# One row list against another: gate products of two chunks read their rows back from DRAM, and fillers, products and route writes change places

## The chip, the cores and the metric

The kernel runs on one core of a Trainium2 chip. The metric is the device time of one launch in microseconds; the median of three runs of the kernel before is 587.76 us (586.64 to 587.94). A profiled execution gives the rows that are read below.

## The reference, cut to what matters

```
phi(x) = exp(x omega^T - |x|^2/2 - max) / sqrt(128)        # q and k, scaled; 4 batches, 8 heads, 576 rows, 64 columns
x      = (phi(q) (phi(k)^T v)) / (phi(q) sum(phi(k)))      # linear attention, 2304 rows of 512
h      = x w_in;  x = (h * clip(h + 3, 0, 6) / 6) w_out    # dense layer, 512 -> 2048 -> 512
score  = x w_skip;  logits = x w_gate                      # 1 + 8 gate products per row
e      = argmax(logits);  p = softmax(logits)[e]
out    = x + p * relu(x w1[e]) w2[e]   where score > 0,    else x
```

## The kernel before

Four batches of attention (pairs of heads, `attention`) make x, transposed, in two parts of rounded floats (`xh` and `xl`). The dense layer goes over five chunks of rows, `CHS = (512, 512, 256, 512, 512)`, and 16 steps f of 128 hidden columns each: the product `mm1` (L710, twelve matmuls), ACT's and DVE's relu6 and splitting (L716 to L731: g, gh, gl), and `mm2` (L741, three matmuls for each 128 rows) into accumulators. While the first chunk runs, ACT and DVE also convert the weights (`cv_*`, L641 to L688), which come in as pairs of words; the remainders of w_in are stored as `wils` and loaded again for the later chunks (`load_wil`, tile wil). Attention of batch 1 stands between the products of the first chunk, that of batches 2 and 3 between those of the second and third.

After a chunk's last step, `after(c)` copies each 128 rows from the accumulator into a row buffer x1 (`x1_copy`, ACT, L747; there are three buffers), stores them twice (`x1_out`, SP: to out and to x1d, a table of rows in DRAM), and takes nine gate products of them on DVE (`gate_dot`, L756: a multiply and sum over 512 columns into lg). Then comes the routing of the chunk (`route_*`; `route_put` writes the route table tab from POOL, L834). With four chunks routed, the expert with the most rows (`group`, steps `ga_*`) and a side block (`s_*`) are worked on, their rows fetched from x1d and their results written by POOL (L910, L933), while the fifth chunk ends.

Nothing of this order is found at run time. Each step is registered by `sc.add` with its engine, a cost, its reads and writes, and the buffers it holds; the string `ORDER` numbers the steps in the order in which `Schedule.run` emits them, and every engine takes its own in that order. On all engines a step waits for the ones before it on the same engine, and for its data and buffers. SP issues most loads and stores in the same way.

One thing is emitted by the way. A step "warm" takes a PSUM bank (`warm.append(pacc())`), and until the step that clears it `warm_up` (L292 to L300) puts filler matmuls on the zero tile idle in front of each PE step: `OPEN = 7` of them (14 matmuls in the trace) until the planner's own gap in front of a step is over 0.1, after that as many as fit into that gap. The fillers have no cost in the planner, and the place of the two steps in `ORDER` is as free as that of any other.

```
for _ in range(int((gap - 0.1) / AT["fill"]) if len(warm) > 1 else OPEN):
    T.matmul(warm[0][:, 0:128], idle, idle, start=True, stop=True)
```

## Time and profile before

| what | before |
|---|---|
| median of 3 runs (lowest, highest) | 587.76 us (586.64, 587.94) |
| the profiled execution's own time, and its span | 585.66 us, 583.7 us |
| mean granted TensorE clock in the span | 0.994 |
| busy: PE, DVE, ACT, POOL | 564.7, 422.1, 292.4, 107.7 us |
| HBM read and written | 61.62 MB, 15.18 MB |

The span goes from the first to the last instruction; the own time has what lies around it as well. A busy engine is not always one that paces the others: PE's matmuls are pipelined, so their durations overlap, and start to start is the measure of its pace. Times in the rows are microseconds from the start of the span.

### The profile page before, as it was taken

The page shows a single profiled execution, that of the slowest core. Times are in us where ns is not written, and L with a number is a line of the kernel's source. Part 1 is how long each engine was busy: PE and PEld are TensorE (multiplying, and loading weights), DVE is VectorE, ACT ScalarE, POOL GpSimd, SP SyncE. Part 2 cuts the span into 40 slices and gives each one's busy share as a digit, 9 for nine tenths or more (in the row PEclk, how much of TensorE's full clock was granted, in tenths as well). Part 3 has the DMA queues.
Part 4 walks back from the last instruction along what each step waited for, and adds up shares of the span by engine and source line. Part 5 has one row for each costly group of instructions (what it writes and reads, how often), then busy time and mean ns, then how long its engine had stood idle before and what let it go on. Part 6 is the DMA issues. An engine that isn't in the chain of part 4 may idle for free. (4 is left out here: it accounts for less than half of the span.)

```text
span 583.7 us, 11120 instructions
## 1 busy us (share of the span) xinstructions
PE 564.7 (97%) x4089; PEld 465.3 (80%) x4089; DVE 422.1 (72%) x1116; ACT 292.4 (50%) x665; POOL 107.7 (18%) x83
## 2 busy tenths in 40 slices
PE   6799999999999999999999999999999999999993
PEld 5678787877888788778988888888888888888882
DVE  4998999899968964539889646134489855589881
ACT  5998999998562343238644332121232323552310
POOL 3550221100200202104432002000010035000263
PEclk9999999999999999999999999999999999999997
DMA  8643566566535034215513322213232245473621
GB/s 314 211 151 131 180 232 201 186 195 215 174 135 173 20 123 148 77 48 177 151 57 106 117 68 73 71 38 90 73 83 86 85 128 164 143 230 100 209 68 74
DMA packets 36103, 77.41 MB, mean 133 GB/s; under 512 B 5484, under 2 KB 6124, under 8 KB 36048
## 3 DMA queue, kind: packets, MB, share of 16 engines
q1 hardware_dynamic: 33872, 72.70, 39.2%
q0 software_dynamic: 1744, 3.56, 1.9%
q8 instruction: 33, 0.54, 0.4%
q10 hardware_dynamic: 432, 0.43, 0.3%
q14 instruction: 22, 0.18, 0.1%
HBM read 61.62 MB, written 15.18 MB: 132 GB/s over the span
## 5 line engine op out<-in xcount | busy, mean ns | idle before, releaser
L741 PE MATMUL acc<-wo,gh 128*128 128x512 f32 x576 | 181.3, 396 | 0.0
L741 PEld LDWEIGHTS acc<-wo,gh 128*128 128x128 f32 x576 | 105.4, 188 | 23.9 <-issue 1.9
L756 DVE CUSTOM_DVE_ANT_0 idle<-x,wg 128x512 uint8<-128x512 f32 x162 | 115.2, 711 | 8.6 <-ACT x L747 4.7
L741 PE MATMUL acc<-wo,gl 128*128 128x512 f32 x288 | 112.3, 390 | 0.0
L716 ACT ACTIVATE g<-mm,half_t 128x512 f32<-128x512 f32 (+1 forms) x80 | 51.3, 646 | 84.0 <-PE mm L710 64.0
L549 POOL PARTITION_ALL_REDUCE mx<-pr x26 | 53.2, 2078 | 216.7 <-ACT pr L541 170.0
L731 DVE TENSOR_TENSOR gl<-g,gh 128x512 fp32r<-128x512 f32 (+1 forms) x80 | 51.7, 647 | 49.2 <-ACT gh L725 35.0
L721 DVE SCALAR_TENSOR_TENSOR g<-g,mm 128x512 f32<-128x512 f32 (+1 forms) x80 | 49.8, 629 | 49.5 <-ACT g L716 49.2
L725 ACT CAST gh<-g 128x512 fp32r<-128x512 f32 (+1 forms) x80 | 46.2, 581 | 76.6 <-PE acc L741 64.4
L710 PE MATMUL mm<-xh,wih 128*128 128x512 f32 (+1 forms) x320 | 80.8, 374 | 0.0
L710 PE MATMUL mm<-xl,wih 128*128 128x512 f32 (+1 forms) x320 | 78.8, 368 | 0.0
L710 PEld LDWEIGHTS mm<-xh,wih 128*128 128x128 f32 x320 | 56.2, 188 | 11.5 <-ACT pr L541 0.4
L710 PEld LDWEIGHTS mm<-xl,wih 128*128 128x128 f32 x320 | 56.8, 188 | 10.2
L741 PEld LDWEIGHTS acc<-wo,gl 128*128 128x128 f32 x288 | 54.1, 188 | 11.7
L710 PE MATMUL mm<-xh,wil 128*128 128x512 f32 (+1 forms) x256 | 61.6, 363 | 0.0
L710 PEld LDWEIGHTS mm<-xh,wil 128*128 128x128 f32 x256 | 44.9, 189 | 7.6
L834 POOL DMA_INDIRECT tab<-rec,r_sloti x18 | 18.7, 1042 | 173.1 <-DVE rec L830 169.2
L468 ACT ACTIVATE kp<-att,kmx 128x128 f32<-128x128 f32 x130 | 39.6, 424 | 16.7 <-DVE kmx L453 16.1
L453 DVE TENSOR_REDUCE kmx<-att 128x3 f32<-128x384 f32 (+1 forms) x64 | 28.5, 481 | 8.1 <-PE att L447 8.0
L666 DVE CUSTOM_DVE_ANT_0 ca<-w,ca 128x1024 uint16<-128x1024 uint16 x32 | 24.5, 769 | 3.2 <-ACT w L652 2.3
L447 PE MATMUL att<-wb,raw 64*128 64x128 f32 x260 | 21.1, 295 | 5.1 <-DVE wb L359 4.4
L447 PEld LDWEIGHTS att<-wb,raw 64*128 64x128 f32 x260 | 18.3, 198 | 9.2 <-DVE wb L359 4.4
(220 smaller groups left out, 770.4 us busy)
## 6 DMA issues: line engine op xcount, KB each, us to landing
wil<-wils SPq DMA_DIRECT2D x64, 256.0 KB, 2.8
w<-w_in SPq DMA_DIRECT2D x16, 512.0 KB, 3.6
w<-w_out SPq DMA_DIRECT2D x16, 512.0 KB, 3.4
out<-x SPq DMA_DIRECT2D x18, 256.0 KB, 3.3
x1d<-x SPq DMA_DIRECT2D x18, 256.0 KB, 3.4
vx<-vn SPq DMA_DIRECT2D x13, 322.5 KB, 4.7
wils<-cl SPq DMA_DIRECT2D x16, 256.0 KB, 4.1
wraw<-w SPq DMA_DIRECT2D x16, 256.0 KB, 3.1
```

Source lines behind the costliest of these rows:

```text
L447: T.matmul(st[key, b, p, g, h][:, i * M:(i + 1) * M], x[half(h), min(c * 128, S - 128):min(c * 128 + 128, S)], wb[half(h), :], start=True, ...
L453: V.reduce_max(out=mx[:, 0:n], in_=st[key, b, p, g, h][:, 0:n * M].rearrange("p (g m) -> p g m", m=M), axis=AX.X, negate=True)
L468: A.activation(kp[:, i], ps[:, i * M:(i + 1) * M], AF.Exp, bias=mx[:, i:i + 1], scale=1.0)
L549: G.partition_all_reduce(mx, st["e", b, p, r], channels=128, reduce_op=bass_isa.ReduceOp.max)
L666: V.tensor_tensor(c, c, lo, op=ALU.add)
L710: T.matmul(po, w[:, k, :], moving(x, k, c), start=(n == 0), stop=(n == 3 * KC - 1))
L716: A.activation(t, mmp[c, f][:, 0:CHS[c]], AF.Relu, bias=half_t, scale=2.0 ** -UP / 6.0)
L721: V.scalar_tensor_tensor(out=t, in0=t, scalar=1.0, in1=mmp.pop((c, f))[:, 0:CHS[c]], op0=ALU.min, op1=ALU.mult)
L725: A.copy(gh, gt[c, f])
L731: V.tensor_sub(gl, t, gh.bitcast(F32))
L741: T.matmul(accs[c, t], g[:, ts], w[:, r, f % 2, :], start=(f == 0 and j == 0), stop=(f == FT - 1 and j == 2))
L756: V.tensor_tensor_reduce(out=idle.bitcast(mybir.dt.uint8), in0=x1[i], in1=wg[:, e, :], scale=1.0, scalar=0.0, op0=ALU.mult, op1=ALU.add, a ...
```

## The change

The gate products of chunks 0 and 1 (`LATE`) no longer read the row buffer that ACT has filled, but one that a new step, `x1_in`, loads back from x1d after `x1_out` has stored the rows. The buffer that ACT filled is free when its two stores have landed, and the gate products may stand at any later place before the chunk's routing. The new list has eight steps more (2091 in place of 2083). It moves these products from the second chunk's steps to the end of the third and into the fourth (chunk 0), and into the fourth (chunk 1), and the routing of the chunks with them. It moves most other steps too.

```diff
+LATE = (0, 1)
...
 ORDER = """
-257 258 295 296 333 334 2 259 297 371 261 17 260 267 273 264 274 262 280 269 275 298 270 281 299 276 302 265 277 372
...
+257 258 295 296 17 0 2 333 334 371 259 260 297 32 264 273 262 265 274 280 261 281 298 275 282 276 299 263 302 372 300
...
+    def x1_in(i):
+        xt = x1p.tile([128, DM], F32, tag="x1", bufs=3, name="x1")
+        nc.sync.dma_start(xt, x1d[i * 128:(i + 1) * 128, :])
+        x1[i] = xt
...
-            sc.add("SP", 2 * SPC, t + 1, lambda i=i: x1_out(i), r=[("x1", i)], o=[("wil", (c + 1, 3 + 2 * k))], w=[("x1d", c)], t=[("x1", i)],
+            sc.add("SP", 2 * SPC, t + 1, lambda i=i: x1_out(i), r=[("x1", i)], o=[("wil", (c + 1, 3 + 2 * k))], w=[("x1d", c), ("x1o", i)], t=[("x1", i)],
                    nbytes=128 * DM * 8)
+            again = c in LATE
+            if again:
+                sc.add("SP", SPC, t + AT["dot"] + k * 9 - 5, lambda i=i: x1_in(i), r=[("x1o", i)], w=[("x1i", i)], t=[("x1", ("i", i))], nbytes=128 * DM * 4)
             for e in range(NE + 1):
-                sc.add("DVE", 0.7, ..., lambda i=i, e=e: gate_dot(i, e), r=[("x1", i), "wg"], w=[("lg", c)],
-                       t=[("x1", i)])
+                sc.add("DVE", 0.7, ..., lambda i=i, e=e: gate_dot(i, e), r=[("x1i" if again else "x1", i), "wg"], w=[("lg", c)],
+                       t=[("x1", ("i", i) if again else i)])
```

Lines of the changed kernel are one higher up to the products, and six higher from the gate products on (L298 is L299, L710 is L711, L834 is L840, L910 is L916).

**The start, on ACT and PE.** ACT's first computing steps (L541 copies a query projection, L468 is an exponential of keys), before:

```order
L541 ACT_TABLE_LOAD
L541 COPY pr<-mm 128x288 x2
L468 ACTIVATE kp<-att,kmx 128x128 x2
L541 COPY pr<-mm 128x288 x2
L468 ACTIVATE kp<-att,kmx 128x128 x6
L541 COPY lent_h<-mm 128x288 x2
```

and now:

```order
L469 ACT_TABLE_LOAD
L469 ACTIVATE kp<-att,kmx 128x128 x3
L542 COPY pr<-mm 128x288 x4
L469 ACTIVATE kp<-att,kmx 128x128 x3
L469 ACTIVATE lent_r<-att,kmx 128x128 x3
L542 COPY lent_h<-mm 128x288
```

PE up to the first product of the first chunk (L590 transposes x, L568 makes numerators, L513 and L447 project queries and keys, L298 is the filler), before:

```order
L590 MATMUL mm<-ident,xn 128x128 x10
L568 MATMUL att<-kv,pr 64x65 x20
L513 MATMUL att<-raw,wb 128x288 x2
L298 MATMUL acc<-idle 128x128 x7
L710 MATMUL mm<-xh,wih 128x512 x4
L710 MATMUL mm<-xl,wih 128x512 x4
L710 MATMUL mm<-xh,cl 128x512 x4
```

and now:

```order
L569 MATMUL att<-kv,pr 64x65 x20
L591 MATMUL mm<-ident,xn 128x128 x5
L514 MATMUL att<-raw,wb 128x288 x2
L448 MATMUL att<-wb,raw 128x128 x12
L514 MATMUL att<-raw,wb 128x288 x2
L711 MATMUL mm<-xh,wih 128x512 x4
L711 MATMUL mm<-xl,wih 128x512 x4
L711 MATMUL mm<-xh,cl 128x512 x4
```

An exponential has moved to the front of ACT's list, and the filler no longer stands in front of the first product; two projections of keys and a query projection stand there instead.

**The fillers, on PE.** In the list before, the row above is the only one of L298. In the new list the rows of the filler stand in the first chunk, between second products (acc<-wo) of its steps:

```order
L569 MATMUL att<-kv,pr 64x65 x20
L742 MATMUL acc<-wo,gh 128x512 x2
L742 MATMUL acc<-wo,gl 128x512
L591 MATMUL att<-ident,xn 128x128 x2
L299 MATMUL acc<-idle 128x128 x7
L742 MATMUL acc<-wo,gh 128x512 x2
L742 MATMUL acc<-wo,gl 128x512
L299 MATMUL acc<-idle 128x128 x7
L742 MATMUL acc<-wo,gh 128x512 x2
L742 MATMUL acc<-wo,gl 128x512
L299 MATMUL acc<-idle 128x128 x7
L514 MATMUL att<-raw,wb 128x288 x4
```

Three blocks of seven are emitted where there was one.

**The end, on POOL.** The last writes, before (L834 the route table, L910 a block's rows, L933 the side block's):

```order
L910 DMA out<-xgb,ga_rec 2304x512 x2
L834 DMA tab<-rec,r_sloti 19456x2 x2
L910 DMA out<-xgb,ga_rec 2304x512
L933 DMA out<-xg,s_rec 9216x128
L910 DMA out<-xgc,ga_rec 2304x512 x2
```

and now:

```order
L840 DMA tab<-rec,r_sloti 19456x2 x2
L916 DMA out<-xgb,ga_rec 2304x512 x2
L916 DMA out<-xgc,ga_rec 2304x512
L840 DMA tab<-rec,r_sloti 19456x2
L916 DMA out<-xgc,ga_rec 2304x512
L939 DMA out<-xg,s_rec 9216x128
```

The side block's write has become the last one, and a write of the route table stands between the last two of the blocks' rows. On PE the side block's last steps (L1185, 64 matmuls in the trace) have moved behind the last products of the group.

## Rows read from the trace of the kernel before

**Rows 1.** Page: busy time, share of the span and instructions of each engine.

```profile
PE 564.7 (97%) x4089; PEld 465.3 (80%) x4089; DVE 422.1 (72%) x1116; ACT 292.4 (50%) x665; POOL 107.7 (18%) x83
```

**Rows 2.** Windows: length, then busy us (x instructions) by engine, clock, DMA share, GB/s.

```profile
15.00:30.00 15.00, 11.55 (x225) 9.44 (x224) 13.86 (x29) 14.26 (x40) 7.13 (x4) 1.00 0.57 196
30.00:45.00 15.00, 14.07 (x268) 11.81 (x266) 13.98 (x36) 15.00 (x48) 7.82 (x4) 1.00 0.47 146
...
75.00:90.00 15.00, 15.00 (x145) 12.24 (x143) 13.75 (x31) 15.00 (x33) 2.93 (x2) 1.00 0.62 206
285.00:300.00 15.00, 14.62 (x162) 12.61 (x159) 13.10 (x34) 8.46 (x25) 6.86 (x3) 1.00 0.35 109
...
360.00:375.00 15.00, 15.00 (x68) 12.43 (x67) 7.60 (x18) 2.90 (x5) 1.97 (x3) 1.00 0.20 52
```

**Rows 3.** Page: the gate products (busy, mean ns); the wil loads (KB, us to landing).

```profile
L756 DVE CUSTOM_DVE_ANT_0 idle<-x,wg 128x512 uint8<-128x512 f32 x162 | 115.2, 711 | 8.6 <-ACT x L747 4.7
...
wil<-wils SPq DMA_DIRECT2D x64, 256.0 KB, 2.8
```

**Rows 4.** Timeline of ACT, 0 to 50 us: start, us, what, idle before.

```profile
7.93 0.70 ACT L541 COPY pr<-mm 128x288 f32<-128x288 f32 x2 [4.30 <-PE mm L513]
...
23.51 2.17 ACT L468 ACTIVATE lent_r<-att,kmx 128x128 f32<-128x128 f32 x8
...
27.81 1.43 ACT L652 ACTIVATE w<-w 128x512 f16<-128x512 f32 x1
...
46.26 0.74 ACT L605 CAST xh<-mm 128x192 fp32r<-128x192 f32 x1
```

**Rows 5.** Timeline of DVE: the last xl of batch 0.

```profile
45.52 2.01 DVE L610 TENSOR_TENSOR xl<-mm,xh 128x384 fp32r<-128x384 f32 x5
```

**Rows 6.** Timeline of PE, 47 to 50 us: the fillers and the first product.

```profile
47.52 1.83 PE L298 MATMUL acc<-idle 128*128 128x128 f32 x14
49.11 1.18 PE L710 MATMUL mm<-xh,wih 128*128 128x512 f32 x4
```

**Rows 7.** Timelines of PE and DVE: the first matmuls, the first maximum.

```profile
4.42 2.50 PE L447 MATMUL att<-wb,raw 64*128 64x128 f32 x20 [4.42 <-DVE wb L359]
5.68 0.42 DVE L453 TENSOR_REDUCE kmx<-att 128x2 f32<-128x256 f32 x1 [1.31 <-PE att L447]
```

**Rows 8.** Timeline of PE, 34 to 41 us: prices of attention steps.

```profile
34.92 0.76 PE L513 MATMUL att<-raw,wb 64*128 64x288 f32 x4
...
38.42 0.94 PE L447 MATMUL att<-wb,raw 64*128 64x128 f32 x12
39.30 0.92 PE L484 MATMUL att<-vx,kp 128*64 128x65 f32 x24
```

**Rows 9.** Timelines of ACT and PE near 82 us: an exponential, its numerator product.

```profile
81.75 0.73 ACT L558 ACTIVATE pr<-pr 128x576 f32<-128x576 f32 x1
83.72 1.39 PE L568 MATMUL att<-kv,pr 128*64 128x65 f32 x40
```

**Rows 10.** Timeline of PE, 102 to 106 us: a visit to a half-width shape.

```profile
102.90 0.39 PE L741 MATMUL acc<-wo,gl 128*128 128x512 f32 x1
103.22 1.39 PE L484 MATMUL att<-vx,kp 128*64 128x65 f32 x40
104.54 0.74 PE L741 MATMUL acc<-wo,gh 128*128 128x512 f32 x2
105.11 0.39 PE L741 MATMUL acc<-wo,gl 128*128 128x512 f32 x1
```

**Rows 11.** Timelines of PE and POOL: the side block and the end.

```profile
555.54 1.96 PE L1185 MATMUL acc<-ew,rT 128*32 128x128 f32 x64
573.98 0.39 PE L1059 MATMUL att<-gw,xl 128*128 128x512 f32 x1
574.07 0.97 POOL L910 DMA_INDIRECT out<-xgc,ga_rec  x1 [0.35 <-DVE xgc L1065]
575.43 0.97 POOL L910 DMA_INDIRECT out<-xgc,ga_rec  x1 [0.39 <-DVEq L1583]
```

More of the change, by code (lines that the diff above doesn't have):

```diff
@@ L1432, in after @@
                    t=[("ps", ("acc", c, k)), ("x1", i)])
-            sc.add("SP", 2 * SPC, t + 1, lambda i=i: x1_out(i), r=[("x1", i)], o=[("wil", (c + 1, 3 + 2 * k))], w=[("x1d", c)], t=[("x1", i)],
+            sc.add("SP", 2 * SPC, t + 1, lambda i=i: x1_out(i), r=[("x1", i)], o=[("wil", (c + 1, 3 + 2 * k))], w=[("x1d", c), ("x1o", i)], t=[("x1", i)],
                    nbytes=128 * DM * 8)
+            again = c in LATE
+            if again:
+                sc.add("SP", SPC, t + AT["dot"] + k * 9 - 5, lambda i=i: x1_in(i), r=[("x1o", i)], w=[("x1i", i)], t=[("x1", ("i", i))], nbytes=128 * DM * 4)
             for e in range(NE + 1):
-                sc.add("DVE", 0.7, t + (AT["dot"] if c != CA - 1 else 0) + k * 9 if c < NCH - 1 else t + AT["dot5"] + k, lambda i=i, e=e: gate_dot(i, e), r=[("x1", i), "wg"], w=[("lg", c)],
-                       t=[("x1", i)])
+                sc.add("DVE", 0.7, t + (AT["dot"] if c != CA - 1 else 0) + k * 9 if c < NCH - 1 else t + AT["dot5"] + k, lambda i=i, e=e: gate_dot(i, e), r=[("x1i" if again else "x1", i), "wg"], w=[("lg", c)],
+                       t=[("x1", ("i", i) if again else i)])
         u = t + AT["route5"] if c == NCH - 1 else t + 25 if c == CA - 1 else t + AT["route"]
```

160 rows, old and new, of the table ORDER are left out of this document.

## The prediction

> **What bounds the kernel now.** I read the engine totals first: TensorE (PE) is busy 564.7 of the 583.7 us of the span, the next engine, VectorE (DVE), 422.1 [rows 1]. A total is a mean over stages, so the windows come second [rows 2]. From 75 to 90 us and from 360 to 375 us PE is busy 15.00 of 15.00. It is not from 15 to 45 us (11.55 and 14.07) and, slightly, from 285 to 300 us (14.62). In the early windows it is ScalarE (ACT) that has no room: 14.26 and 15.00 of 15.00 between 15 and 45 us, and 15.00 again from 75 to 90. So the time is made of four things: when PE can begin the products of the first chunk, how much PE work is still to do then, what is added to PE's stream or taken from it after that, and what follows PE's last matmul. From 360 to 375 us that stream holds 68 matmuls of 512 columns in 15.00 us, about 0.225 us each, 2.7 us for a product of twelve.
>
> The gate products are on DVE: 162 of 0.71 us, 115.2 us [rows 3]. Nothing on PE waits for them before the routing, and DVE is busy 7.60 of 15.00 from 360 to 375 us [rows 2]. Moving them later is by itself priced at nothing; the work of PE hides it as long as DVE keeps below 15 in the windows that receive them. What decides is the order on PE, ACT and POOL that came with it.
>
> **Term 1, the first product: -2.5 us.** Before, ACT starts at 7.93 us and runs, nearly without a gap, to the last xh copy at 47.00 [rows 4]; the last xl of DVE ends at 47.53 [rows 5]. The first product starts only at 49.11, because 14 filler matmuls on idle, listed in front of it, begin at 47.52 and take 1.59 us [rows 6]. In the changed list no filler stands there. The ACT work ahead of the last xh copy is also smaller: eight exponentials fewer (eight take 2.17 us) and one L652 more (1.43 us with an overlap of some 0.3 with the next), so 1.0 us less [rows 4]. And ACT's first step is now an exponential of the three-chunk half. Before, PE does the two-chunk half first (8 of the 20 matmuls in 2.5 us), and DVE's first maximum starts at 5.68, some 0.3 us after it, and takes 0.42 [rows 7]. In the changed list the 12 matmuls of the three-chunk half come first, until about 5.8, the maximum follows near 6.1 and takes some 0.5, and ACT starts near 6.9 instead of 7.93. Walking down ACT's new list with these durations I find one new gap, about 1.2 us near 10 us, where the next exponential waits for the next pair's maximum. The last xh copy then ends near 45.2. Four PE steps stand between the last transpose and the first product, so it starts near 46.6, and 49.11 - 46.6 = 2.5. The bounds: -4.4 if ACT has no gap and PE follows at once, and -1.0 if only the filler goes and part of that is lost again.
>
> **Term 2, work done ahead of it: -0.5 us.** Of PE's 53 steps up to the first product the changed list has one more key projection (12 matmuls, 0.94 us), one more query projection (4, 0.76 us) and one k-v product fewer (24, 0.92 us) [rows 8]. That is 0.8 us with the overlaps at their ends; the two projections stand beside others of their shape, so I take 0.5, between 0.3 and 0.8.
>
> **Term 3, new waits for ACT in the first chunk: +1.0 us.** In the changed list four products of 2.7 us stand almost back to back at the start, so PE runs ahead of ACT. For the numerator product of pair 2 of batch 1 the old list has 66 ACT instructions between the last xh copy and the exponential that it needs, the new one 81; PE's own work up to there grows by 4.2 us. In its full window ACT does 33 instructions in 15.00 us [rows 2], so fifteen are 6.8 us, 2.6 more than 4.2. Before, that exponential ended near 82.4 and PE came at 83.72, a margin of 1.3 us [rows 9]. The margin less 2.6, and less 0.7 for the earlier first product, would be a wait of 2.0 us. Where ACT had idled before for want of PE's results the new work fits into the gaps, and the wait would be 0. I take the middle.
>
> **Term 4, the fillers: +4.8 us.** The filler rule emits seven instructions, 14 matmuls in the trace, before each PE step from the one that takes the filler's bank until the clear. In the changed list these two stand in the middle of the first chunk, and three blocks of seven come out, between products of L742 (the order shown with the change). 3 x 1.59 = 4.8 us [rows 6]. PE is busy 15.00 of 15.00 there, so nothing hides them; only a wait of PE that they replace could. The block removed in front of the first product is already in term 1. The lower bound is 2.8, if 2 us of waits for ACT fall behind them.
>
> **Term 5, changes of the array's shape: -1.9 us.** The attention matmuls use half the rows or half the columns of the array, and a visit to one costs more than its matmuls. Around the visit at 103.22 the matmul before it takes 0.32 us instead of 0.225, and the first two after it take 0.57 instead of 0.45; with about 0.06 at the exit that is 0.27 [rows 10]. After the first product the old list returns 28 times from such a visit to a full product, the new one 21 times: 7 x 0.27 = 1.9 (1.1 to 2.5).
>
> **Term 6, the late waits: -0.4 us.** PE's idle time from 285 to 300 us is 15.00 - 14.62 = 0.38 us [rows 2], where DVE is at 13.10 with the attention of batch 3 and the gate products of the second chunk. In the new list DVE has less to do ahead of 270 us. I take the whole of it, with +2 as the other bound: the gate products that now stand from 345 to 435 us bring DVE near 15 of 15 there.
>
> **Term 7, the end: +1.0 us.** Before, PE's last matmul starts at 573.98, and POOL's last write runs from 575.43, 1.45 us later, to 576.40: 2.42 us after that matmul [rows 11]. The changed list ends PE with the eight small steps of the side block (64 matmuls, 1.96 us). Behind the last large product POOL then has four writes in a row: a block's rows, one of the route table, a block's rows, the side block. Each takes 0.97 us, and they follow each other every 1.3 us or so (574.07, 575.43). With the first at 1.45 us after the product before the last, the fourth ends some 6.2 us after it, and PE's own last matmul starts 2.8 us after it. That leaves 3.4 us in place of 2.42. Bounds: 0 and +1.5.
>
> **Reloads: 0.** Eight loads of 256 KB are added on SP's queue. A load of that size (wil, the stored remainders) takes 2.8 us to land [rows 3]; the rows were stored long before. Behind a waiting reload on SP stand the next wil loads, and a product waits for those; they would be PE's next wait (a rival below).
>
> **The sum.** -2.5 - 0.5 + 1.0 + 4.8 - 1.9 - 0.4 + 1.0 = +1.5 us. The profiled execution's own time was 585.66 us, of which 583.7 are the span; the median of the three runs shown is 587.76, 2.1 higher. The terms are differences, so I put them on the median: **589.2 us**, slower by 0.25%. About 0.2%, 1.2 us, is what a measurement of this kernel can tell from no change.
>
> **The rivals.**
>
> *ACT runs through without a gap* (faster, 0.17). If the 1.2 us gap near 10 us does not open and PE is ready when the last xl lands, the first product starts at 44.7 and term 1 is -4.4; PE then meets a filled ACT list and term 3 is 0. The sum is -4.4 - 0.5 + 4.8 - 1.9 - 0.4 + 1.0 = -1.4: 586.4 us. For it: ACT is busy 15.00 of 15.00 from 30 to 45 us [rows 2]. Against it: only 14.26 in the window before, where the first maxima and reductions are waited for. It decides from a first product before 45 us.
>
> *ACT paces the whole first chunk* (no change, 0.14). Then the fillers stand where PE would have waited and cost nothing of their own, and the time up to the second chunk is ACT's work, the same in both lists. The gains of term 5 there are lost too. What is left is about -1.0 from the earlier ACT start, -0.4 and +1.0: 587.4 us. For it: ACT's 15.00 from 75 to 90. Against it: PE was busy 15.00 in that window too [rows 2].
>
> *A reload holds SP's queue* (slower, 0.12). Reloads need one of three row buffers, which a store must release. While one waits, the wil loads behind it wait, and PE with them. PE's work between such a load's place in the list and its product, counted in the third chunk with the durations above, is often only some 3 us, little over the 2.8 us of a landing. If five products lose 0.6 us each, the time is 592.2.
>
> *The clock falls without the filler* (slower, 0.04). The granted clock stayed at 1.00 from 15 to 30 us although PE idled 3.45 us there in pieces [rows 2]. The Trainium skill (TensorE: Matmul & The Clock Gate, Why this matters for your kernels) asks that bursts of matmuls have no long idle gaps between them, or the engine drops to half its rate; by that rule taking the filler away from the first product is a risk, by the row it is none. At 1.2 instead of 2.4 GHz that product would take 2.7 us more: 591.9.
>
> **How the numbers follow.** The forecast's case has 0.53, with an own range of 587.6 to 591.0: slower 0.31, within the bound 0.19, faster 0.03. The first rival gives 0.14 faster and 0.03 within, the second 0.14 within, the last two 0.16 slower. Together: faster 0.17, same 0.36, slower 0.47. The range, 585.6 to 592.0, takes in the first two rivals and the bounds of terms 3 and 6, and leaves out the slow rivals' upper halves.
>
> **What would show it.** Right: the first product near 46.6 us with no L299 in front of it; three blocks of 14 L299 matmuls, some 1.6 us each, between products of L742; short waits of PE for pr, lent or gl between 60 and 85 us; POOL's end some 3.4 us after PE's last matmul starts. Wrong: a first product before 45 or after 48; idle time of PE right in front of the fillers (they would then cost less than 4.8); waits of PE for wil in the third chunk, or for gl from 345 to 435 us.

## The result and the profile after

| what | before | after |
|---|---|---|
| median (lowest, highest) | 587.76 us (586.64, 588.4) | 592.8 us (591.39, 593.3) |
| the profiled execution's own time, and its span | 585.66, 583.7 us | 591.53, 589.7 us |
| mean granted TensorE clock | 0.994 | 0.988 |

The ratio of five timed runs each is 1.0081, with an interval of [1.0061, 1.0101]: slower by 5.0 us on the medians, 5.9 us between the profiled executions. The prediction said 589.2, and its range ended at 592.0. The direction was right, the size was not.

The page after, the lines that answer to [rows 1] and [rows 3]:

```profile
PE 568.7 (96%) x4117; PEld 470.7 (80%) x4117; DVE 424.3 (72%) x1116; ACT 293.0 (50%) x665; POOL 108.1 (18%) x83
...
L762 DVE CUSTOM_DVE_ANT_0 idle<-x,wg 128x512 uint8<-128x512 f32 x162 | 114.4, 706 | 6.7 <-ACT x L748 2.8
...
wil<-wils SPq DMA_DIRECT2D x64, 256.0 KB, 2.7
```

PE has 28 matmuls more and 4.0 us more of busy time; 28 are two blocks of fillers. The gate products cost what they did, and a wil load still lands in 2.7 us. The windows that answer to [rows 2], and three more (90, 300 and 315 us):

```profile
15.00:30.00 15.00, 13.28 (x210) 10.56 (x212) 14.35 (x30) 13.66 (x39) 7.15 (x5) 0.77 0.57 199
30.00:45.00 15.00, 13.83 (x288) 11.59 (x285) 14.55 (x34) 14.97 (x43) 7.08 (x4) 1.00 0.37 121
75.00:90.00 15.00, 15.00 (x144) 12.23 (x142) 14.52 (x30) 14.93 (x34) 2.95 (x2) 1.00 0.74 225
90.00:105.00 15.00, 15.00 (x95) 12.46 (x93) 9.12 (x17) 9.91 (x23) 3.91 (x2) 1.00 0.39 121
285.00:300.00 15.00, 14.89 (x178) 13.46 (x177) 7.73 (x21) 9.06 (x28) 4.69 (x3) 1.00 0.57 170
300.00:315.00 15.00, 14.38 (x121) 11.76 (x120) 12.74 (x32) 6.26 (x16) 4.20 (x3) 1.00 0.53 158
315.00:330.00 15.00, 14.63 (x128) 12.92 (x127) 14.42 (x40) 4.70 (x11) 3.29 (x2) 1.00 0.33 94
360.00:375.00 15.00, 15.00 (x69) 12.28 (x68) 8.38 (x29) 3.21 (x5) 0.00 (x0) 1.00 0.27 83
```

Three things are to be seen. The clock is 0.77 in the mean from 15 to 30 us, where it was 1.00: PE is busy longer there, and its matmuls are slower (shown below). The idle time from 285 to 300 us fell from 0.38 to 0.11 us, and 0.62 and 0.37 us stand in the next two windows. From 90 to 105 us PE is full while ACT and DVE are not. That is where the fillers are, in the timeline of PE:

```profile
48.59 1.20 PE L711 MATMUL mm<-xh,wih 128*128 128x512 f32 x4
...
90.91 1.73 PE L299 MATMUL acc<-idle 128*128 128x128 f32 x14
...
93.18 1.72 PE L299 MATMUL acc<-idle 128*128 128x128 f32 x14
...
95.44 1.72 PE L299 MATMUL acc<-idle 128*128 128x128 f32 x14
```

The first product starts at 48.59, 0.5 us before [rows 6], and three blocks of fillers have come. The end, on PE and on POOL, against [rows 11]:

```profile
574.75 0.39 PE L1065 MATMUL acc<-gw,xl 128*128 128x512 f32 x1
575.07 1.69 PE L1191 MATMUL acc<-ew,rT 128*32 128x128 f32 x38
577.22 0.27 PE L1191 MATMUL acc<-ew,rT 128*32 128x128 f32 x1 [0.46 <-issue]
...
579.35 0.42 PE L1191 MATMUL acc<-ew,rT 128*32 128x128 f32 x4 [1.01 <-issue]
...
580.78 0.67 PE L1191 MATMUL acc<-ew,rT 128*32 128x128 f32 x16 [0.41 <-issue]
```

```profile
578.31 0.97 POOL L916 DMA_INDIRECT out<-xgc,ga_rec  x1 [0.30 <-issue]
582.12 0.97 POOL L939 DMA_INDIRECT out<-xg,s_rec  x1 [2.84 <-DVE xg L944]
```

The 64 small matmuls of the side block took 6.1 us from the start of the first to that of the last, in pieces with idle time between them that nothing in the profile explains ("issue"). POOL stood 2.84 us for them before its last write. In [rows 11] the same 64 are one piece of 1.96 us, some 1.7 from first to last start. All times of this block below are from first to last start.

Term by term, from the two traces, the 6.0 us of the span are:

| term | forecast | measured |
|---|---|---|
| 1, first product | -2.5 | -0.5 |
| 2, work done ahead of it | -0.5 | -0.8 |
| 3, waits for ACT in the first chunk | +1.0 | 0 |
| 4, fillers | +4.8 | +4.6 |
| 5, changes of shape | -1.9 | -1.4 |
| 6, late waits | -0.4 | +1.15 |
| 7, end | +1.0 | +4.0 |
| other | 0 | -1.05 |

Term 7 is the time from the last large product's start to the end of POOL's last write, 8.34 us instead of 2.42, less the 1.88 us of side block matmuls that moved there and are missing elsewhere. "Other" is 0.35 us in small pieces and 0.7 us of span behind POOL's last write. Terms 2 and 5 measure -2.2 together; of that, 0.8 is the price of the moved steps by [rows 8], an estimate. A second profile of the kernel after, on another chip (the run of 589.73 us below), has the same stream of PE to 0.05 us between the first product and the last large one, but its first product starts at 49.95, 0.8 us later than in [rows 6], and its term 7 is +1.5. So terms 2 to 6 repeat, and the two ends do not.

### The profile page after: what moved, and what is told of

Same layout as the page of the kernel before. It is cut to its first block, busy times and chain, and to the rows that moved or that the text cites. A ratio compares the mean times of both kernels' runs of the same rounds, so it can differ in the third digit from the quotient of the medians.

```text
span 589.7 us, 11212 instructions
## 1 busy us (share of the span) xinstructions
PE 568.7 (96%) x4117; PEld 470.7 (80%) x4117; DVE 424.3 (72%) x1116; ACT 293.0 (50%) x665; POOL 108.1 (18%) x83
## 5 line engine op out<-in xcount | busy, mean ns | idle before, releaser
L732 DVE TENSOR_TENSOR gl<-g,gh 128x512 fp32r<-128x512 f32 (+1 forms) x80 | 53.5, 670 | 55.8 <-ACT gh L726 30.9
L711 PE MATMUL mm<-xh,wih 128*128 128x512 f32 (+1 forms) x320 | 80.8, 374 | 1.1 <-ACT pr L542 0.6
L711 PE MATMUL mm<-xl,wih 128*128 128x512 f32 (+1 forms) x320 | 78.8, 368 | 0.0
L711 PEld LDWEIGHTS mm<-xh,wih 128*128 128x128 f32 x320 | 56.1, 188 | 13.3 <-ACT pr L542 0.8
L711 PEld LDWEIGHTS mm<-xl,wih 128*128 128x128 f32 x320 | 56.9, 188 | 10.2
L711 PE MATMUL mm<-xh,wil 128*128 128x512 f32 (+1 forms) x256 | 61.6, 363 | 0.0
L711 PEld LDWEIGHTS mm<-xh,wil 128*128 128x128 f32 x256 | 44.9, 189 | 7.5
L840 POOL DMA_INDIRECT tab<-rec,r_sloti x18 | 19.9, 1105 | 152.4 <-DVE rec L836 148.5
L448 PEld LDWEIGHTS att<-wb,raw 64*128 64x128 f32 x260 | 20.1, 197 | 9.3 <-DVE wb L360 4.4
L448 PE MATMUL att<-wb,raw 64*128 64x128 f32 x260 | 22.6, 296 | 5.0 <-DVE wb L360 4.4
L555 DVE TENSOR_TENSOR pr<-pr,mx 128x576 f32<-128x576 f32 x26 | 21.4, 833 | 6.2 <-POOL mx L550 6.2
```

Of the source, the lines that this page charges most:

```text
L448: T.matmul(st[key, b, p, g, h][:, i * M:(i + 1) * M], x[half(h), min(c * 128, S - 128):min(c * 128 + 128, S)], wb[half(h), :], start=True, ...
L555: V.tensor_sub(pr, pr, st.pop(("qm", b, p, r)))
L711: T.matmul(po, w[:, k, :], moving(x, k, c), start=(n == 0), stop=(n == 3 * KC - 1))
L732: V.tensor_sub(gl, t, gh.bitcast(F32))
```

## The experiments

Each ratio is to the kernel before on the same chip. The runs were made in groups, each on a chip of its own, which turned out to matter for both ends of the program; the chips are numbered here in that order.

### The fillers

Theory: three blocks instead of one are most of the slowdown, and nothing hides any of the four. Rival: the block in front of the first product kept PE ready, and its removal costs as much as it saves. The same edit in both kernels:

```diff
-OPEN = 7
+OPEN = 0
```

In the kernel after:

> The changed kernel with OPEN = 0: the three blocks of 14 filler matmuls in the first chunk are left out, nothing else. Theory (fillers are work on TensorE that nothing hides: ACT is idle 5.1 us and DVE 5.9 of the 15.00 us from 90 to 105 us in the changed kernel's trace, and PE runs 15.00): 4.6 us less, median about 588.2, and the products behind them start 4.6 us earlier. Rival 1 (they stand where PE would have waited for ACT, which is at 14.93 of 15.00 from 75 to 90 us): 0 to 2 us less, 591 to 593, and PE waits for gh or pr between 90 and 110 us. Rival 2 (they keep the granted clock up): more time, clock below 1.00 after 90 us.

Measured: 584.37 us, ratio 0.9965 [0.9952, 0.9977]. In the kernel before:

> The kernel before with OPEN = 0: the block of 14 filler matmuls in front of the first product is left out. Theory (the last xl lands at 47.53 us, so the product could start near 47.6 in place of 49.11): 1.5 us less, about 586.3, if what follows on PE is not waiting for ACT; granted clock unchanged at 1.00. Rival 1 (ACT paces the first chunk): the first product starts 1.5 us earlier, but waits of PE from 50 to 90 us take it back: 587.5 to 588. Rival 2 (the filler keeps the clock up): a stretch at 0.5 near 50 us, and 588 or more.

Measured: 584.02 us, ratio 0.9952 [0.994, 0.9965], the lowest ratio of all runs. PE from the last transposes to the first product, without the block, and the row of the transposes with it, which belongs ahead of [rows 6]:

```profile
44.75 1.33 PE L590 MATMUL mm<-ident,xn 128*128 128x128 f32 x10
...
48.41 1.20 PE L710 MATMUL mm<-xh,wih 128*128 128x512 f32 x4
```

```profile
43.85 1.31 PE L590 MATMUL mm<-ident,xn 128*128 128x128 f32 x10
```

PE has no idle time on this path in either kernel. From the start of the transposes to the first product it takes 3.66 us without the block and 5.26 with it, so the block's 1.6 us are gained in full there. The first product starts only 0.7 us earlier than in [rows 6], because the transposes start 0.9 us later in this run: its clock was half from 32 to 36 us (below). The run of the old list on the same chip that has the block and the same half clock starts its first product at 50.25, 1.84 us later than this one. The 0.48% of the ratio (0.35 to 0.60) are 2.8 us; what the block costs beyond its 1.6 us stays open.

The kernel after and the same without fillers, together on the third chip:

> The changed kernel once more, as it is, on the same chip as the three runs beside it. The slow pieces of the side block's last matmuls (L1191, 6 us in place of 1.7) were there in every run of one set (six fillers, padded start, the old front) and in none of the other set (no fillers, side earlier, side last in the list before), and each set ran on one chip. Theory (they belong to the chip or its state, not to the list): all four kernels of this set that end with the side block show the same, slow or not. Rival (they belong to the list): slow here and in the repeat of the kernel with six or no fillers as they were. In numbers for this kernel: with the slow pieces 1.008 of the kernel before, without them about 1.004.

> The changed kernel with OPEN = 0 once more. Theory (fillers are 4.4 us of work that nothing hides, and the slow pieces belong to the chip): 4.4 us, 0.0075, under the changed kernel beside it; L1191 slow if it is slow there. Rival (leaving the fillers out also ended the slow pieces): L1191 takes 1.7 us here and 6 us in the changed kernel beside it, and 6.8 us less.

Measured: 589.73 us, 1.0053 [1.004, 1.0066], and 584.58 us, 0.997 [0.9958, 0.9982]. The three blocks are worth 5.15 us, which is 0.83% in ratios. The change is slower by 0.53% there with the fillers as they are. Without fillers on either side, 0.9970 against 0.9952 (0.9965 against 0.9952 on the first chip), it is 0.18% slower, less than the intervals tell apart. So about 0.35 of the 0.53% are fillers (0.83 less 0.48). One filler less in each block, on the second chip:

```diff
-OPEN = 7
+OPEN = 6
```

> The changed kernel with OPEN = 6: each of the three blocks is 12 matmuls in place of 14. Theory (the slow last 64 matmuls hang on where they lie in TensorE's program, since they ran at full speed with the blocks left out, and a shift by a few instructions moves them): L1191 takes about 1.7 us, and the time is 0.7 + some 2.5 us less than the changed kernel's, about 1.0025 of the kernel before. Rival (they hang on what runs beside them at that moment): L1191 still takes about 6 us in pieces, and the time is 0.7 us less, about 1.007 of the kernel before.

Measured: 591.69 us, 1.0078 [1.0063, 1.0093], with a side block that still took 6.2 us (574.58 to 580.81). This one was meant for the end, to shift PE's later work by less than a microsecond; the slow pieces did not depend on it.

### The end

Theory: the side block's place at the end of the list costs the time, by the queue of POOL's writes behind it and by its slow matmuls. Its last steps earlier in the kernel after, on PE (the moved rows of DVE and POOL are of the same kind):

```diff
 L1065 MATMUL att<-gw_6068,xl 128x512
+L1191 MATMUL acc<-ew_5867,rT 32x128 x16
+L1191 MATMUL acc<-ew_6141,rT 32x128 x16
...
 L1065 MATMUL acc<-gw_6122,xl 128x512
-L1191 MATMUL acc<-ew_5867,rT 32x128 x16
-L1191 MATMUL acc<-ew_6141,rT 32x128 x16
```

> The changed kernel with the side block's eight last steps (64 matmuls), its weighing and its write moved in front of the products of the last group's steps, as the list before has them; fillers, front and reloads stay. Theory (the side block's matmuls are slow because they are the last ones on PE: 6.1 us in place of 1.9, in pieces of about 0.7 us with PE idle): L1191 takes about 1.9 us, POOL's last write ends some 2 to 3 us after PE's last matmul starts, median 588 to 589, 4 to 5 us less. Rival (POOL's queue of writes sets the end: seven writes of 1.3 us from 570.6 us): L1191 short, but POOL's last write ends near 580 to 581; 2 us less, about 590.8.

Measured: 590.26 us, 1.0064 [1.0051, 1.0077]. The side block took 1.68 us, and POOL's last write ended at 581.5, 4.3 us after PE's last matmul had started. That is the rival: in this list the queue of POOL is the bound behind PE's end with the side block earlier, too, and the ratio is no lower than the kernel after's own without slow pieces (1.0053, third chip). The opposite, the eight side steps moved behind the last products in the kernel before, twice:

```diff
-2015 2016 2017 2018 2019 2020 2021 2022
...
+2015 2016 2017 2018 2019 2020 2021 2022
```

> The kernel before with the side block's last eight steps put behind all other products, its weighing and write last on DVE and POOL; nothing else moves. Theory (being last makes these matmuls slow): L1185 takes about 6 us, in pieces with PE idle, and the end comes 4 to 6 us later: 592 to 594. Rival 1 (the slow pieces belong to something else in the changed kernel's end, such as POOL's writes beside it): L1185 takes 1.9 us, and the end comes 0.5 to 1.5 later: 588.3 to 589.3.

> The kernel before with the side block's last steps behind all other products, once more. If the slow pieces belong to the chip: L1185 takes 6 us here if L1191 does in the changed kernel beside it, and the time is some 1.004 to 1.005 of the kernel before; if not, 1.001 as on the first chip. If they belong to the list: L1185 takes 1.7 us whatever the others show, 1.001.

Measured: 586.77 us, 1.0009 [0.9999, 1.0018], and 586.45 us, 1.0006 [0.9996, 1.0016]: no difference that can be told, with the side block at 1.68 us both times. (In both, a wait of PE of 1.5 or 1.6 us for gw of DVE came with it.) So its place alone makes no slow pieces and no difference in the total that can be told, though POOL's last write ended at 577.42 in the second, 1.0 us later than in [rows 11]. The kernel after itself had no slow pieces either on the third chip (the run of 589.73 us above), on PE and on POOL:

```profile
576.08 0.39 PE L1065 MATMUL acc<-gw,xl 128*128 128x512 f32 x1
576.40 1.96 PE L1191 MATMUL acc<-ew,rT 128*32 128x128 f32 x64
```

```profile
578.37 0.97 POOL L840 DMA_INDIRECT tab<-rec,r_sloti  x1 [0.30 <-issue]
579.65 0.97 POOL L916 DMA_INDIRECT out<-xgc,ga_rec  x1 [0.30 <-POOLq L1592]
580.92 0.97 POOL L939 DMA_INDIRECT out<-xg,s_rec  x1 [0.30 <-issue]
```

Three writes follow each other every 1.28 us, and the last ends at 581.89, 3.8 us after PE's last matmul started (576.40 + 1.68), where the prediction had 3.4. That is term 7 as it was thought of. On the second chip the slow pieces were there in all three kernels that end with the side block: the one with six fillers above, and two more. One of these has idle matmuls on 32 columns at the start of the program:

```diff
-OPEN = 7
+OPEN = 0
...
+    spare = psum.tile([128, 512], F32, tag="ps", bufs=8, name="spare")
+    for _ in range(21):
+        T.matmul(spare[:, 0:32], idle, idle[:, 0:32], start=True, stop=True)
```

> The changed kernel with OPEN = 0 and, at the very start of TensorE's program, 21 narrow matmuls on idle (32 columns), as many as the three blocks held: behind the first chunk the program lies as in the changed kernel, and the matmuls run while TensorE still waits for its first operands. Theory (place in the program): the slow pieces of L1191 are back, 6 us, and the time is some 2.5 us over that of the kernel with OPEN = 0, about 1.001 of the kernel before. Rival (what runs beside them): L1191 takes 1.7 us and the time is that of the kernel with OPEN = 0, 0.9965 of the kernel before.

Measured: 593.06 us, 1.0100 [1.0086, 1.0115], and a side block of 6.0 us. The idle matmuls took 9.17 us and moved the first projection from 4.4 to 10.15 us and the first product to 54.07, so the ratio says nothing of the end; the row of the side block does. That the place in the program makes the pieces was my next theory. The front of the kernel before (its first 230 steps), with the rest of the kernel after, ends with the same instructions as the kernel after without fillers:

> The first 230 steps in the order of the kernel before (up to the first product), the rest in the order of the changed kernel, OPEN = 0. Beside the changed kernel with OPEN = 0 this undoes the front alone. Theory (the new front gains nothing: it has VectorE's last xl as late as before, and its clock falls to half from 15 to 22 us): the first product starts at 47.6 to 48.4 in place of 49.11, no half clock before 22 us, some work that the new front had done ahead comes later (0.8 us), and the time is 0 to 1 us less than with the new front: 0.995 to 0.9965 of the kernel before. Rival (the new front is worth the 2.5 us that I forecast, and something behind it hides that): 1 to 2.5 us more, about 0.999.

Measured: 587.97 us, 1.0011 [1.0003, 1.002]. PE's end, of this kernel and then of the kernel after without fillers on the third chip:

```profile
571.30 1.57 PE L1191 MATMUL acc<-ew,rT 128*32 128x128 f32 x41
573.29 0.27 PE L1191 MATMUL acc<-ew,rT 128*32 128x128 f32 x1 [0.41 <-issue]
...
576.84 0.86 PE L1191 MATMUL acc<-ew,rT 128*32 128x128 f32 x14 [0.99 <-issue]
```

```profile
571.43 1.95 PE L1191 MATMUL acc<-ew,rT 128*32 128x128 f32 x64
```

The same 64 matmuls at the same time of the program take 6.0 and 1.7 us. The theory of the place falls. With the slow pieces in it, this ratio says nothing of the front, for which the run was meant as well. The pieces come with the chip, its state or the single run, and not with the list: they were in the first profile of the kernel after and in the three of the second chip, and in none of the others, on four chips. What PE lacked in the gaps stays open. A mended end, in the kernel after without fillers: the side steps earlier as above, and three writes of the route table in front of the first of the blocks' rows on POOL.

```diff
+2085 2083 2084
...
+2022
...
-2085
...
-2083
...
-2022
...
-2084
```

> The changed kernel with OPEN = 0, the side block's last eight steps in front of the last group's products as in the list before, and the three writes of the route table moved in front of the first result's write on POOL, where POOL waits 6.0 us. Theory (POOL's queue, with ten entries of 1.3 us each behind that wait, sets the end in the changed list): POOL's last write ends some 2.5 us after PE's last matmul starts in place of 5.8 after the last L1065 (3.8 after PE's last matmul), 1.4 us less than with OPEN = 0 alone where L1191 is fast, 4 us less where it is slow: about 0.993 to 0.994 of the kernel before. Rival (the last products set the end): no gain beside the kernel with OPEN = 0, 0.9965.

Measured: 584.39 us, 0.9967 [0.9956, 0.9978], beside 584.58 without the mend. POOL ended at 576.05 instead of 576.91. The 0.9 us are in the trace and not in the ratio, which is the rival's.

### The start and the clock

The front of the kernel after (235 steps) with the rest of the kernel before, without fillers, on the second chip:

> The first 235 steps in the order of the changed kernel (up to the first product), the rest in the order of the kernel before, no reloads, OPEN = 0. Beside the kernel before with OPEN = 0 this brings in the new front alone. Theory (the new front is worth 0 or a little less): the clock is half for some 7 us near 15 to 22 us, first product near 48.6 to 49.1, the work done ahead gives 0.8 us back, and the time is 0 to 1 us over that of the kernel before with OPEN = 0, 0.995 to 0.997 of the kernel before. Rival (the new front is worth 2.5 us): about 0.991.

Measured: 587.2 us, 0.9996 [0.9987, 1.0005]. The first product started at 48.51, the clock was half from 15 to 22 us as in the kernel after, and one new wait came, of PE for DVE:

```profile
61.70 0.73 PE L741 MATMUL acc<-wo,gh 128*128 128x512 f32 x2 [0.89 <-DVE xl L610]
```

Neither value came: 0.9996 is 0.44% over the kernel before without its filler (0.9952, first chip), with the first product at almost the same time (48.51 and 48.41). In the two profiles the last large product starts 2.0 us later; 0.89 of it is this wait, 0.57 a side block of 2.26 us, which on this chip had one gap of 0.3 us in it. The rest is open, and so is the price of the front in the total.

The half clock is in all eleven profiles with the front of the new list and nothing added to it; it begins between 15 and 19 us (at 24 in the run with the idle matmuls at the start) and lasts 3 to 7 us. It is not a matter of that list alone. Of the seven profiles with the old front, with and without the filler, four have a clock of 0.51 to 0.71 from 32 to 34 us and three have 1.00, among them the kernel before's own, and PE was busy 1.24 or 1.25 and then 1.31 or 1.32 of 2.00 just ahead of that in all seven. So the same list had it in one run and not in the next. With the block of fillers in place, the first product starts at 49.11 and 48.97 without the half clock, at 50.25 and 50.14 with it: 1.0 to 1.3 us. The 86 timed runs of the kernel before fit that: on each of the five chips those whose mean granted clock is below 0.994 (45 runs) are 0.8 to 1.2 us longer in the mean than the others.

What PE did before the clock fell, in windows of 2 us of the kernel after:

```profile
10.00:12.00 2.00, 1.74 (x9) 1.00 (x8) 2.00 (x6) 1.95 (x8) 2.00 (x2) 1.00 1.04 408
12.00:14.00 2.00, 1.97 (x17) 1.48 (x16) 1.76 (x4) 2.00 (x7) 1.30 (x2) 1.00 1.05 421
14.00:16.00 2.00, 1.34 (x4) 0.29 (x2) 1.91 (x3) 2.00 (x6) 2.00 (x2) 0.80 1.03 405
16.00:18.00 2.00, 1.32 (x2) 0.50 (x2) 1.97 (x3) 1.89 (x6) 1.37 (x1) 0.50 0.54 212
```

A mean of 0.80 from 14 to 16 us puts the fall at about 15.2. One wait of 0.65 us for ACT stands right ahead of it; the next two, of 0.58 and 0.55 us, stand behind it, and the work between them runs at the 1.2 GHz level, 0.50 of 2.4:

```profile
14.92 1.07 PE L514 MATMUL mm<-lent_h,wb 64*128 64x288 f32 x2 [0.65 <-ACT lent_h L542]
16.57 1.32 PE L514 MATMUL mm<-lent_h,wb 64*128 64x288 f32 x2 [0.58 <-ACT kp L469]
18.45 2.79 PE L448 MATMUL att<-wb,lent_h 64*128 64x128 f32 x20 [0.55 <-ACT lent_r L469]
```

The 20 matmuls of L448 take 2.79 us where 20 of them took 1.48 at 19.83 us in the kernel before. To keep the clock, 11 idle matmuls (22 in the trace) behind the query projections in question, into columns that these leave free:

```diff
-OPEN = 7
+OPEN = 0
...
+KEEP = {(0, 1, 0, 1): 1, (0, 1, 1, 1): 1, (0, 2, 0, 1): 3, (0, 2, 1, 0): 3, (0, 2, 1, 1): 3}
...
+                for _ in range(KEEP.get((b, p, i, r), 0)):
+                    T.matmul(ps[r][:, 384:512], idle, idle, start=True, stop=True)
```

> The changed kernel with OPEN = 0 and 11 matmuls on idle behind query projections of the first batch (unused columns of the same bank), 22 in the trace, at TensorE's short waits between 10 and 18 us, so that it idles less before the clock falls. Theory (the waits bring the half clock from 15 to 22 us, and that costs ScalarE two waits of 0.8 and 0.4 us near 21 and 22.6 us): the clock stays at 1.00 to 25 us, ScalarE's last xh ends about 1.2 us earlier and the first product starts at 47.6 to 48.1 in place of 49.1: 0.9945 of the kernel before. Rival 1 (VectorE's list sets the end of the start: its last xl): clock kept, first product within 0.3 us of 49.1, 0.9965. Rival 2 (the matmuls are themselves in the way): clock kept, first product later than 49.3, 0.997 or more.

Measured: 583.79 us, 0.9959 [0.9945, 0.9972]. The clock stayed, and the first product came at 48.34; in the two runs of the kernel after without fillers it came at 49.11 and 49.29 (first and third chip):

```profile
16.00:18.00 2.00, 2.00 (x13) 1.50 (x14) 1.97 (x3) 1.84 (x5) 1.61 (x1) 1.00 0.56 213
18.00:20.00 2.00, 1.69 (x20) 1.49 (x20) 2.00 (x4) 2.00 (x9) 0.38 (x1) 1.00 0.00 0
...
48.34 1.21 PE L714 MATMUL mm<-xh,wih 128*128 128x512 f32 x4
```

The price of the clock is less sure than these numbers. With this front and the half clock the first product lies anywhere from 48.51 to 49.95 (ten profiles); in the only other run that kept the clock (all mends together, below) it lies at 48.77. Pairs on the same chip, without and with the idle matmuls, are 49.65 and 48.34 (fourth) and 49.06 and 48.77 (fifth): 1.3 and 0.3 us. Against 0.9965 and 0.997 without the idle matmuls the total is not told apart. ACT's wait of 0.81 us near 21 us stayed too: it is not the clock's.

### The gate products

The title of the change is their move, and the prediction priced it at nothing. In the kernel before, filler kept, only the reloads, the gate products of the first two chunks and what depends on them, stood beside the products of TensorE that they stand beside in the kernel after:

```diff
+LATE = (0, 1)
...
+            again = c in LATE
...
-                sc.add("DVE", 0.7, ..., lambda i=i, e=e: gate_dot(i, e), r=[("x1", i), "wg"], w=[("lg", c)],
+                sc.add("DVE", 0.7, ..., lambda i=i, e=e: gate_dot(i, e), r=[("x1i" if again else "x1", i), "wg"], w=[("lg", c)],
```

> The list of the kernel before with the named change alone: the rows of chunks 0 and 1 are loaded back, and their gate products, the routing of chunks 0 to 2 and the copies of chunk 2's rows stand at the places between TensorE's products that the changed list gives them; all else, the filler too, in the old order. Theory (the reloads are hidden and VectorE has room at the later places): 0.998 to 1.002 of the kernel before; no wait of TensorE for wil. Rival 1 (a reload that waits holds SP's queue, and products wait for wil): 1.002 to 1.006 with waits for wil in the third and fourth chunk. Rival 2 (VectorE's gate products stand in the way of attention's last steps near 300 to 320 us): waits of TensorE for xn, gl or pr there of 0.5 to 2 us.

Measured: 597.25 us, 1.019 [1.0176, 1.0204]. And without the filler:

> The same list as the run with the named change alone, with OPEN = 0. Theory (the filler block of the old list is worth 1.5 to 2 us, the late gate products nothing): 0.9952 of the kernel before, as with the old list and OPEN = 0. Rival: what that run loses comes on top: 0.997 to 1.001.

Measured: 594.56 us, 1.0136 [1.0121, 1.0152]. PE waits 6.9 us in five for gl in the first of these, 5.9 in four in the second, and in both 1.4 us for g and 1.1 for gh, which the kernel before does not have. What DVE does in front of one of them, and PE's wait for it:

```profile
345.91 0.69 DVE L762 CUSTOM_DVE_ANT_0 idle<-x,wg 128x512 uint8<-128x512 f32 x1
346.53 0.68 DVE L722 SCALAR_TENSOR_TENSOR g<-g,mm 128x512 f32<-128x512 f32 x1
347.13 0.41 DVE L732 TENSOR_TENSOR gl<-g,gh 128x256 fp32r<-128x256 f32 x1
```

```profile
347.60 0.50 PE L742 MATMUL acc<-wo,gl 128*128 128x512 f32 x1 [1.65 <-DVE gl L732]
```

Eight gate products of 0.69 us run in one row there, from 340.79 on, and g and gl, which PE wants, stand behind them. The longest wait, 2.00 us at 445.53, stands behind a row of routing steps, which moved with them. No wait of PE was for wil, so the reloads cost it nothing that the traces show. So "priced at nothing" holds for the place that the new list gives these products, between other work, and not for the move as such. My placement was crude, by PE's products alone; what the best one would bring was not tried. In the kernel after, one such collision is left, with the gap on PE:

```profile
318.06 0.69 DVE L762 CUSTOM_DVE_ANT_0 idle<-x,wg 128x512 uint8<-128x512 f32 x1
319.17 0.56 DVE L582 TENSOR_TENSOR xn<-att,rd 128x384 f32<-128x384 f32 x1
```

```profile
319.78 0.74 PE L711 MATMUL mm<-xh,wih 128*128 128x256 f32 x4 [0.37 <-DVE xn L582]
```

Two runs tried to remove it, by gate products moved behind the xn step in the kernel after without fillers. The first took five of them, behind the wrong xn:

```diff
-1634 1646
...
-1639
...
-1629
...
-1658
...
+1634 1646 1639 1629 1658
```

> The changed kernel with OPEN = 0, and five gate products of chunk 0 behind the division (rd, xn) that TensorE waits for near 315 us (319.78 us in the changed kernel) in place of ahead of it. Theory (TensorE's wait of 0.53 us there comes from these gate products): the wait is gone, 0.5 us less than with OPEN = 0, which the times can hardly tell: 0.996 of the kernel before. Rival (xn is late for another reason): the wait stays, 0.9965.

Measured: 586.28 us, 0.9999 [0.999, 1.0009], 0.3% over the kernel after without fillers on the third chip: the gap stayed, and the five products in a row made a new wait:

```profile
333.06 0.74 PE L711 MATMUL mm<-xh,wih 128*128 128x256 f32 x4 [1.50 <-DVE g L722]
```

The second took four others:

```diff
-1615
...
-1642 1620
...
-1614
...
+1615 1642 1620 1614
```

> The changed kernel with OPEN = 0, and the four gate products that stand on VectorE right in front of the division of 384 columns (rd, xn) behind it. The run before this one had moved five others, which stand later. Theory (TensorE's wait near 315 us for the bank that this xn frees comes from them): the gap of 0.76 us between two matmuls there falls to some 0.3 or less, all else as with OPEN = 0, 0.996 of the kernel before. Rival (xn is late for another reason): the gap stays at 0.76 us, 0.9967. Rival 2 (what comes behind them is late in its turn, as in the run before): another wait of 0.5 us or more on VectorE's g or gl from 315 to 345 us, 0.997 to 1.000.

Measured: 584.61 us, 0.9966 [0.9953, 0.9978]. The gap for xn was gone, and one of 0.85 us came near 319.47, partly for ACT's pr: what is late next stood right behind it. At last the three mends together, clock, end and xn:

> The changed kernel with OPEN = 0, the matmuls that keep the clock at the start, the side block's steps and POOL's writes as in the run with the mended end, and the division ahead of its gate products. Theory (they add up): the clock is 1.00 throughout, first product near 48.3 us, POOL's last write near 574.8 us, 0.994 to 0.995 of the kernel before. Rival (the end takes it back, since with the mended end alone 0.9 us came out of it): 0.9955 to 0.9965.

Measured: 584.25 us, 0.9963 [0.9949, 0.9976], first product at 48.77, clock 1.00 up to PE's end, POOL's end at 575.72. The rival's value came: the mends do not add up to a total that can be told. It beats both kernels, but not the kernel before without its filler (0.9952), from which it is not told apart.

## Why the prediction was off

**Term 1 is the one whose step failed in the reasoning.** The forecast hung the first product on ACT's last xh copy, at 45.2, with four PE steps in some 1.4 us behind it. ACT did much as it was told: it starts at 6.72 (6.9 was said), does 52 exponentials instead of 60, and its last xh ends earlier than before, at 46.47. The 1.6 us of the old block were right as well. Three things were not. First, the gaps of ACT: the one of 1.2 us that was foreseen near 10 us is 0.12 us in this profile (0.94 in the second one), and others came:

```profile
6.72 0.88 ACT L469 ACTIVATE kp<-att,kmx 128x128 f32<-128x128 f32 x3 [3.09 <-DVE kmx L454]
...
21.70 0.88 ACT L469 ACTIVATE lent_r<-att,kmx 128x128 f32<-128x128 f32 x3 [0.82 <-DVE kmx L454]
...
22.99 0.27 ACT L499 COPY kv<-acc 128x130 f32<-128x130 f32 x1 [0.41 <-PE acc L485]
...
45.77 0.70 ACT L606 CAST xh<-mm 128x192 fp32r<-128x192 f32 x2 [0.38 <-PE mm L591]
```

Behind ACT's start, 1.6 us of idle time stand in these rows, and xh ends at 46.47 in place of 45.2. Second, DVE: 83 instructions stand in front of its last xl, in place of 78, and it ends at 47.79, later than before [rows 5]:

```profile
46.98 0.81 DVE L611 TENSOR_TENSOR xl<-mm,xh 128x384 fp32r<-128x384 f32 x2
```

Third, PE itself. Its last transposes wait for xn of DVE and start at 45.32, where those of the kernel before start at 43.85:

```profile
45.32 0.41 PE L591 MATMUL mm<-ident,xn 128*128 128x128 f32 x2 [0.28 <-DVE xn L582]
```

From there to the first product PE has no idle time: two query projections and a key projection fill 3.27 us, and the product waits neither for xh nor for xl. The profiles of this front with the clock kept have the same 3.27 us (45.07 to 48.34), and so has the second one of the kernel after (46.68 to 49.95). So the path to the first product goes through ACT and DVE in turn (14.97 and 14.55 of 15.00 from 30 to 45 us) up to the last transposes and then through PE's own list, and a shorter list on ACT moves little. The 0.5 us gained in the first profile became 0.8 us lost in the second, so the gain is not one of the list. The half clock, which no term has, is a part of it and not the whole: with the clock at 1.00 the first product still stands at 48.34 and 48.77, not at 46.6.

**Term 7 had the right mechanism and missed the most in size.** On the third chip POOL's end comes 3.8 us after the side block's last matmul, near the 3.4 said. What the sum did not have is that this block itself can take 6.1 us, 2.5 of the term's 4.0 us in the first profile. Only the runs showed it, and what makes it stays open. That the comparison gave 1.0081 with the slow pieces and 1.0053 on the third chip without them fits that, though the two intervals overlap a little. On the third chip the change cost 3.4 us, where the forecast had 1.5 and its range ended at 4.2; so how far off the forecast was depended on the chip.

**Term 4 was right, the largest term.** 4.61 us from start to start, and the runs gave 5.15 us for all. Nothing hid them: ACT and DVE were at 9.91 and 9.12 of 15.00. Its other half, that the old block's removal from the first product is worth 1.6 us, was right too: 5.26 us from the transposes to the product became 3.66.

**Term 5 was right in size.** The seven visits saved gave 1.4 us of the 1.9, by the sums of PE's times from start to start on product and attention lines, less the waits and the estimate of term 2.

**Term 3 was a wait that did not come.** No wait of PE for ACT stands from 50 to 240 us. PE was not as early as forecast, 2.0 us later at the first product.

**Term 6 had the wrong sign.** The 0.38 us from 285 to 300 fell to 0.11, as said, and gaps of 0.51, 0.90 and 0.76 us from one start to the next at 239.99, 300.59 and 319.02 took its place. The second is a wait for pr of ACT and the third one for xn, behind moved gate products; for the first the profile names nothing. That was inside the bound of +2. The run that cleared the gap for xn got another one in its place, so it is the order of single steps that decides here.

**The rivals.** No gapless ACT, no pacing of the whole chunk by ACT, no reload that holds SP: no wait for wil is in the trace, and the loads land in 2.7 us. The clock did fall, but from 15 to 22 us, not at the first product, where the kernel before without its filler had 1.00 from 36 us on. Its cost, 0.3 to 1.3 us at the first product, was in no term. The row that I put against this rival (3.45 us of idle time at a clock of 1.00) was one execution's: four other profiles of the same front have a half clock from 32 us on, shortly behind that window. The Trainium skill (TensorE: Matmul & The Clock Gate, Why this matters for your kernels) warns of long idle gaps between bursts of matmuls. Here the trace goes beyond that warning: the clock fell without a long gap, for from PE's first matmul to the fall at 15 us none was longer than 0.65 us. So short gaps were not safe in this kernel. Idle matmuls in the short gaps held the clock at 1.00 in both runs that had them.

## What to carry to other kernels

Filler matmuls that a rule emits into a full stream cost their whole length, so look where the rule puts them after every change of the order: here three blocks cost 5.15 us, and taking them out was the only edit whose gain can be told. When a start is paced by several engines in turn, walk every list that leads to the first product, TensorE's own too, with the waits between them, before a gain on one is counted. Moved work that is "hidden" is hidden instruction by instruction: eight 0.69 us products in a row cost PE 1.65 us in one wait, on an engine that was busy 12.46 and 12.28 of 15.00 us in the two windows around it. And one profile is one execution: the first product of the same kernel stood at 48.59 and at 49.95.

## What was not expected of the hardware

The same 64 matmuls on 32 columns at the end of the program took 1.7 us on four chips and 6.0 to 6.2 us on another, in pieces with gaps of 0.3 to 1.1 us for nothing that the profile shows. The kernel after had both, 6.1 and 1.7 us, in two profiles. In the place that the kernel before gives it, the block took 1.7 and, on the chip of the slow pieces, 2.26 us. What makes the gaps is open.

The granted clock of one and the same list was half for some us at the start of one execution and not of another, with the same busy time of PE ahead of it, and it fell without an idle gap of PE longer than 0.65 us (the kernel after).

POOL's last indirect writes take 0.97 us each and follow each other every 1.28 us, rows and route table alike. A queue of them behind the last product set the end of this program.
